# Query block loads moved to the GpSimd queue, and the last sixteen output stores spread over three queues

## The chip, the cores and the metric

The kernel runs on one core of a Trainium2 chip. The metric is the device time of one execution in microseconds (us), and the median of several executions is compared. The engines named below are PE (TensorE; PEld is its weight load), DVE (VectorE), ACT (ScalarE), POOL (GpSimd) and SP (SyncE). SP computes nothing in this kernel: it issues transfers. SPq, ACTq and POOLq are the instruction queues of those engines, on which transfers are issued in program order.

## What is computed

Two blocks in sequence, all in float32. A decayed linear attention over blocks of 64 positions, 4 batches of 8 heads, 768 positions, head dimension 64:

```
intra = einsum('bhic,bhjc->bhij', qb, kb) * Dmask      # Dmask from lam
intra = einsum('bhij,bhjd->bhid', intra, vb)
inter = einsum('bhid,bhde->bhie', qb * lam_pow, kv_state)
out[block] = intra + inter
kv_state = lam_block * kv_state + einsum('bhsd,bhse->bhde', kb * rev_pow, vb)
```

Its output, as 3072 tokens of 512 values, goes through two matrix products with a leaky relu between them:

```
h = x @ w_in                # 512 -> 2048
g = maximum(0.01 * h, h)
y = g @ w_out               # 2048 -> 512
```

The two weights arrive as 64-bit floats and are converted on the chip.

## The kernel before

**Tiling.** The attention is cut in 24 chunks of 128 positions of one batch, 6 chunks to a batch. Four chunks are a group of 512 tokens, so there are six groups. A round (`round_of`, L538) does one chunk: transposes or loads of transposed keys and queries, the scores, the state update, the outputs, and the split of the result in three float32r parts, from which `up` (L697) forms the first product of a group by blocks of 256 columns. Each single float32 product is built of three matmuls on such parts. The results of `up` pass through ACT twice (L727 and L732), are partly combined on DVE (`sums`, L760) and stored to DRAM buffers `g` and `b` (L738, L774) by way of two SBUF buffers `gs`. A buffer `gs` can be written again only when its stores have landed. Later, the second product (L834) reads these DRAM buffers back, and PE runs it from about 310 us to the end.

**Loads of the later chunks.** The first ten chunks (0 to 9) load keys and queries with whole rows (`load_kq`, L339) and transpose them on PE. From chunk `DV` = 10 on, `load_subs` (L371) brings keys and queries of a run of chunks in 32 x 32 blocks, and `turn` (L386) transposes the blocks on DVE (L391). A run is two chunks (10 and 11) or three (12, 15, 18 and 21 onwards), five runs in all. Of each run, keys and queries take 16 transfers each: four indexes `y` of a pair of heads, four quarters `a` of the partitions. One such transfer fills 32 partitions, with pieces of 128 bytes: 48 KB in 384 pieces for a run of three chunks, 32 KB for a run of two. The queries of runs 10, 15, 18 and 21 go to the former query buffer in `att`; those of run 12 to `w32` and `lows`, which other work uses before and after. A run's queries may overwrite the buffer only when `turn` has read the last chunk of the run before. All these loads were issued by SyncE, at L382.

**The order of the work.** The order of each engine's instructions is made by a planner before the program is built (`Plan`, L37). `add` takes an operation with its engine, an assumed duration, keys that it reads and writes, and a rank. `emit` (L83) goes through an assumed time line, always taking the operation that could start first and, among equals, the lowest rank, and issues the instructions in that order. It keeps one assumed clock for each engine, with SP's transfers under the name "DMA". An operation's result counts as available after its duration, a lag for its engine (`LAG`: 3.5 for "DMA", 0.12 for "POOL") and, where `plan.slack` is set, that slack. `move` (L287) adds a transfer to the "DMA" engine with a slack of 1.0 in the earlier part and 4.0 in the steady part (runs 18 and 21 are planned there). In the steady part a block load counts 0.75 (`SUBL`) and before it 0.55. On the chip the instructions of one engine's queue run in this order, and a waiting instruction holds back those behind it.

**The other work of POOL.** In the attention, POOL scales the keys (L427), scales the queries (L431) and decays the state between blocks (L470).

**The output.** `turn_out` (L898) transposes a result bank on DVE (L902) into `otile`, which lies over `gs`, and `store_out` (L905) writes it with four transfers, one for each quarter of the partitions (L910). Before the last bank, these are issued on ACT's queue. At the very end, for the last group, a call is made for banks 2 and 3 (`cs[0]` is 2), both halves `m`, and then, bank 1 being done in two halves, a call for banks 0 and 1 for each half. That is 16 stores of 64 KB, 256 pieces of 256 bytes each. These alternate between SP and ACT.

Of the kernel before, what the change touches and what calls it, by code (L numbers as in the profile page):

```python
# [25 lines left out]
S = 4096.0  # L26
# [5 lines left out]
def _bc(ap, idx, n):  # L32
    a = [list(x) for x in ap.ap]
    return bass.AP(ap.tensor, ap.offset, a[:idx] + [[0, n]] + a[idx:])


class Plan:  # L37
# [23 lines left out]
    def add(self, eng, us, fn, reads=(), writes=(), rank=0.0):  # L61

        n, deps = len(self.ops), set()
        for k in reads:
            w, r = self.last.setdefault(k, [None, []])
            if w is not None:
                deps.add(w)
            r.append(n)
        for k in writes:
            w, r = self.last.setdefault(k, [None, []])  # L70
            if w is not None:
                deps.add(w)
            deps.update(r)
            self.last[k] = [n, []]
        deps.discard(n)
        ways = {eng: us} if isinstance(eng, str) else dict(zip(eng, us))
        if self.slack:
            self.more[n] = self.slack
        if self.chain is not None:
            self.chains[self.chain].append(n)  # L80
        self.ops.append((ways, fn, deps, (self.rank + rank, n), set(writes)))
# [81 lines left out]
def kernel(  # L163
# [10 lines left out]
    nc = tc.nc  # L174
    P = 128
# [18 lines left out]
    SLACK, GSLACK = 4.0, 2.0  # L194
# [5 lines left out]
    LEAD = 8.0  # L200
    WSLACK = 5.0
    DV = 10
    RUNS = {10: (-8.0, 0.8), 12: (4.0, 0.0)}
    C4 = P // 4
    HALF = (slice(0, D), slice(D, 2 * D))
# [72 lines left out]
    plan = Plan()  # L278
    plan.idle, plan.spare, plan.warm = busy, "b10", 1.3 + 0.22 * WARM
    add = plan.add  # L280
    steady = False

    def length(us, issue=0.5):

        return issue if steady else us

    def move(us, fn, reads, writes, issue=0.5, rank=0.0, slack=SLACK):  # L287

        plan.slack = slack if steady else EARLY_SLACK
        if steady and not rank:  # L290
            rank = FIRST
        add("DMA", length(us, issue), fn, reads, writes, rank=rank)
        plan.slack = 0.0


    def factors_k():
        for i in range(2):
            nc.vector.tensor_copy(lam_h[:, i * HP:(i + 1) * HP], lam_b[:, i::2])
        nc.vector.tensor_tensor(eye, ident[:, 0:C2], ident[:, C2:C], op=ALU.add)
        for hi in range(2):  # L300
            for hp in range(HP):
                nc.vector.tensor_tensor_scan(decay[:, hi, hp, :], _bc(lam_h[:, 2 * hp + hi], 1, C2), eye, 0.0,
                                             op0=ALU.mult, op1=ALU.add)
# [9 lines left out]
    lam_c = pow_q[:, :, C2 - 1]  # L313
    plan.rank = -1.0
    add("DVE", 1.95, factors_k, [], ["fk", "sc"])
    add("DVE", 1.25, factors_q, [], ["fq"])
    ENG = {"ACT": nc.scalar, "DVE": nc.vector, "POOL": nc.gpsimd}
# [16 lines left out]
    def of(c):  # L334
        return c // NCB, c % NCB, c % 2
# [3 lines left out]
    def load_kq(c):  # L339
        b, n, i = of(c)  # L340
        for src, x, nm in ((k, 0, "k"), (q, 1, "q")):
            y, dst = src[b, :, n * C:(n + 1) * C, :], kqv[x][i]

            def go(y=y, dst=dst):
                for z in range(2):
                    nc.sync.dma_start(out=dst[:, z * HP:(z + 1) * HP, :], in_=y[z::2].rearrange("h p d -> p h d"))
            if nm == "k" or c < DV:
                move(1.15, go, [], [f"{nm}{i}"], issue=1.0)

    def run(c):  # L350

        lo = max(DV, c - c % TURN)
        return lo, c - c % TURN + TURN - lo

    def subs(first, n):


        n = n * C
        def rows(x, lo, hi):
            return x[:, :(hi - lo) * n].rearrange("p (y t) -> p y t", t=n), lo, hi  # L360
        ks = [(*rows(raw[-2], 0, 2), [f"raw{NRAW - 2}"]), (*rows(raw[-1], 2, 4), [f"raw{NRAW - 1}"])]
        qs = [(*rows(kqv_f[1], 0, HP), ["q0", "q1"])]

        if first == DV:
            ks = [(*rows(raw[0], 0, HP), ["raw0"])]
        elif first < DV + TURN:
            qs = [(*rows(w32f, 0, 2), ["w320", "w321"])] + [
                (*rows(lows[i].bitcast(F32), 2 + i, 3 + i), [f"low{i}"]) for i in range(2)]
        return ks, qs

    def load_subs(c):  # L371
        b, n, i = of(c)
        count = run(c)[1]
        for nm, src, pieces in zip("kq", (k, q), subs(c, count)):
            for sub, lo, hi, keys in pieces:
                add("POOL", 0.0, lambda: None, [], keys, rank=-30.0)
                for y in range(lo, hi):
                    for a in range(4):
                        h = y // 2 + (2 * y + a // 2) % HP * 2
                        z = src[b, h, n * C:(n + count) * C, a % 2 * C4:(a % 2 + 1) * C4]  # L380
                        o = sub[a * C4:(a + 1) * C4, y - lo, :]
                        move(0.55, lambda o=o, z=z: nc.sync.dma_start(  # L382
                                out=o.rearrange("j (m i) -> j m i", i=C4), in_=z.rearrange("(m j) i -> j m i", j=C4)),
                            keys, [f"{nm}s{y}{a}"], issue=SUBL, rank=RUNS.get(c, (4.0, 0.4))[0] + RUNS.get(c, (4.0, 0.4))[1] * (4 * y + a))

# [13 lines left out]
    def transposes(c):  # L399
# [9 lines left out]
        def go(src, at):  # L409
            for y in range(HP):  # L410
                nc.tensor.transpose(out=at[y], in_=src[:, 2 * y:2 * y + 2, :].rearrange("p a d -> p (a d)"), identity=ident)  # L411

        if c < DV:
            add("PE", 0.44, lambda: go(tk, at), [f"k{i}"], [key])
            add("PE", 0.44, lambda: go(tq, [pt[:, y, :] for y in range(HP)]), [f"q{i}"], ["pt"])

        def copies():
            kT = kTs[i]
            into = kT if c < GC else kT.rearrange("p (t a) x -> p t (a x)", t=2)
            src = z if c < GC else z.rearrange("p t a x -> p t (a x)")  # L420
            if c < DV:
                add("ACT", 0.6, lambda: nc.scalar.copy(into, src), [key], [f"kT{i}"])
# [115 lines left out]
    def round_of(c):  # L538

        after = []  # L540
        if c + 2 < NCH:
            load_kq(c + 2)
        plan.begin(c)

        if c < 2 * GC:
            after.append(transposes(c + 2))
        after.insert(0, outputs(c, lambda: after.append(scores(c + 1)) if c + 1 < NCH else None))
        if 2 * GC <= c < NCH - 2:
            after.append(transposes(c + 2))
        plan.end()  # L550
        for x in after:
            x()
        if DV < c + 3 < NCH:
            turn(c + 3)
        if DV + TURN < c + 4 < NCH and (c + 4) % TURN == 0:
            load_subs(c + 4)
        if c + 2 < NCH:
            load_v(c + 2)
# [302 lines left out]
    def plain(pr, p, gi, lead, last=False, banks=None):  # L861
# [20 lines left out]
        for i, c in enumerate(banks):  # L882
            d, b = BANKS[gi][c]
            parts_ = 2 if end and i == 3 else 1
            for half in range(parts_):
                k = ACC[d][b] + (f"half{half}" if parts_ > 1 else "")
                n = T // parts_
                add("PE", 0.227 * 6 * (1.0 if parts_ == 1 else 0.53), lambda c=c, half=half, n=n: go((0, 1), (c,), half * n, n),
                    reads + ([ACC[d][b]] if parts_ > 1 else []), [k])
                turn_out(c, acc[d][b], [ACC[d][b], k], half * n, n)  # L890
                if i == 3 or end and i == 1:
                    cs = sorted(banks[:2] if end and i == 1 else banks[2:] if end else banks)
                    for m in ([half] if parts_ > 1 else range(2)):
                        store_out(pr, gi, m, cs, end)
# [10 lines left out]
    def store_out(pr, gi, m, cs, last):  # L905
        t0, n, w = (2 * pr + m) * T + gi * HT, HT // C4, len(cs) * C4

        def store(a, q):
            c0 = a * P + cs[0] * C4
            q.dma_start(out=out[t0:t0 + HT, c0:c0 + w].rearrange("(b i) j -> i b j", i=C4),  # L910
                        in_=otile[a * C4:(a + 1) * C4, m * n:(m + 1) * n, cs[0]:cs[-1] + 1, :].rearrange("i b c j -> i b (c j)"))

        for a in range(4):
            e = "DMA" if last and (a + m) % 2 else "ACT"
            add(e, 0.5, lambda a=a, e=e: store(a, nc.scalar if e == "ACT" else nc.sync), [f"o{c}{m}" for c in cs], [], rank=-1.5 if last else 6.0)

    def copy_banks(d, s):
        for i in range(2):
# [54 lines left out]
    for n, x in enumerate(seq):  # L973
        plan.rank = float(n)
        steady = begin <= n and x[0] in ("r", "up", "wo")
        if x[0] in "abr":
            {"a": alone, "b": begun, "r": round_of}[x[0]](x[1])
        elif x[0] == "ls":
            load_subs(DV)
            turn(DV)  # L980
        elif x[0] == "lt":
# [59 lines left out]
```

## Time and profile before

| | us |
|---|---|
| median of 3 executions | 606.53 (605.56 to 606.61) |
| the profiled execution, its own time | 606.94 |
| its span, first to last instruction | 605.2 |

All the lines below are of that one profiled execution. Its time is 1.74 us above its span (606.94 - 605.2) and 0.41 us above the median. In the views, a row of the windows gives a stretch of the span, its length, then the busy time of each engine with its count of instructions, the granted TensorE clock (1.00 is full), the mean busy share of the 16 DMA engines and the GB/s moved. A row of the timeline gives the start, the duration, the engine, the line and the operation, with the number of instructions merged, and in brackets how long the engine was idle before it and what ended that. The chain of waits gives start, duration and the work that set the end at that moment.

Of the transfers, `q1` (SP's queue) moved 113.28 MB and `q10` (ACT's) 5.77 MB. No transfer was issued by POOL.

### The profile page before, as it was taken

The page shows a single profiled execution, that of the slowest core. Times are in us where ns is not written, and L with a number is a line of the kernel's source. Part 1 is how long each engine was busy: PE and PEld are TensorE (multiplying, and loading weights), DVE is VectorE, ACT ScalarE, POOL GpSimd, SP SyncE. Part 2 cuts the span into 40 slices and gives each one's busy share as a digit, 9 for nine tenths or more (in the row PEclk, how much of TensorE's full clock was granted, in tenths as well). Part 3 has the DMA queues.
Part 4 walks back from the last instruction along what each step waited for, and adds up shares of the span by engine and source line. Part 5 has one row for each costly group of instructions (what it writes and reads, how often), then busy time and mean ns, then how long its engine had stood idle before and what let it go on. Part 6 is the DMA issues. An engine that isn't in the chain of part 4 may idle for free.

```text
span 605.2 us, 13193 instructions
## 1 busy us (share of the span) xinstructions
PE 589.9 (97%) x5340; PEld 487.4 (81%) x5340; DVE 387.6 (64%) x534; ACT 290.0 (48%) x458; POOL 86.2 (14%) x90
## 2 busy tenths in 40 slices
PE   7899999999999999999999999999999999999996
PEld 6678888888878877887888888888888888888885
DVE  5899765334436327526579858975779595788741
ACT  4678974445555455555577654431344233252300
POOL 1564423104224003202200000000000000000000
PEclk9899999999999999999999999999999999999998
DMA  9999876668899887999879826535467546394533
GB/s 205 226 260 240 254 174 163 158 139 224 207 224 265 216 230 210 216 247 264 266 249 347 260 77 209 167 104 163 148 180 239 176 140 190 121 266 152 174 105 69
DMA packets 190189, 119.89 MB, mean 198 GB/s; under 512 B 128944, under 2 KB 168112, under 8 KB 190128
## 3 DMA queue, kind: packets, MB, share of 16 engines
q1 hardware_dynamic: 176928, 113.28, 66.7%
q10 hardware_dynamic: 13200, 5.77, 3.8%
q8 instruction: 42, 0.69, 0.5%
q14 instruction: 19, 0.16, 0.1%
HBM read 79.17 MB, written 39.85 MB: 197 GB/s over the span
## 4 chain that ended last, share of the span: by engine, by line
PE 89%; DMA 5%; DVE 1%; ACT 1%; SPq 1%; issue 0%; POOL 0%; DVEq 0%; ACTq 0%
PE b L709 38%; PE b L834 13%; PE po L834 13%; PE psc L834 11%; PE pt L834 4%; PE psc L321 4%; PE po L321 4%; DMA b<-gs 2%; DMA raws<-in_moe_w_out_dram 1%; SPq L382 1%; DMA att<-in_v_dram 1%; PE pt L411 1%; DMA att<-in_k_dram 1%; PE po L411 0%; PE b L274 0%
## 5 line engine op out<-in xcount | busy, mean ns | idle before, releaser
L709 PE MATMUL b<-xh,wh 128*128 128x512 f32 (+2 forms) x392 | 103.7, 387 | 2.2 <-ACT gs L732 1.4
L709 PE MATMUL b<-xm,wm 128*128 128x512 f32 (+2 forms) x392 | 104.1, 392 | 1.3 <-ACT b L727 1.3
L709 PE MATMUL b<-xl,wl 128*128 128x512 f32 (+2 forms) x392 | 103.7, 388 | 0.0
L811 ACT ACTIVATE xh<-xm 128x1024 fp32r<-128x1024 f32 x45 | 47.8, 1061 | 91.2 <-DMA xm<-g 39.0
L709 PEld LDWEIGHTS b<-xh,wh 128*128 128x128 f32 x392 | 72.7, 188 | 18.5 <-ACT gs L732 2.7
L709 PEld LDWEIGHTS b<-xm,wm 128*128 128x128 f32 x392 | 71.3, 188 | 17.2 <-ACT b L727 2.5
L709 PEld LDWEIGHTS b<-xl,wl 128*128 128x128 f32 x392 | 72.6, 188 | 14.9 <-DVE wl L614 0.2
L732 ACT ACTIVATE gs<-b 128x512 f32<-128x512 f32 (+2 forms) x97 | 56.9, 590 | 54.3 <-PE b L709 36.5
L727 ACT ACTIVATE b<-b 128x512 f32<-128x512 f32 (+2 forms) x97 | 56.0, 581 | 49.1 <-PE b L709 48.9
L814 DVE SCALAR_TENSOR_TENSOR xl<-xm,xh 128x1024 fp32r<-128x1024 f32 x45 | 54.8, 1218 | 30.8 <-ACT xh L811 26.6
L818 DVE SCALAR_TENSOR_TENSOR xm<-xl,xh 128x1024 fp32r<-128x1024 f32 x48 | 58.7, 1224 | 3.3
L470 POOL TENSOR_TENSOR att<-att 128x256 f32<-128x256 f32 x40 | 34.1, 853 | 54.4 <-DVE att L467 54.4
L602 DVE TENSOR_SCALAR w<-w 128x512 int32<-128x512 int32 x32 | 18.1, 566 | 35.0 <-ACT w L596 34.9
L431 POOL TENSOR_TENSOR att<-att 128x512 f32<-128x512 f32 (+1 forms) x20 | 25.8, 1293 | 95.7 <-DVE att L391 53.5
L460 DVE TENSOR_TENSOR att<-psc,att 128x512 f32<-128x512 f32 x24 | 16.5, 689 | 30.4 <-PE psc L321 30.2
L603 DVE CUSTOM_DVE_ANT_0 w<-w,lows 128x1024 uint16<-128x1024 uint16 x32 | 27.8, 868 | 12.4 <-ACT lows L600 11.2
L321 PEld LDWEIGHTS po<-att 64*64 64x64 f32 x1472 | 27.5, 136 | 8.8 <-issue 5.8
L427 POOL TENSOR_TENSOR att<-att 128x512 f32<-128x512 f32 (+1 forms) x23 | 26.4, 1146 | 57.2 <-DMA att<-in_k_dram 40.2
L321 PE MATMUL po<-att 64*64 64x64 f32 x1472 | 33.2, 224 | 0.6 <-ACT att L499 0.3
L834 PE MATMUL b<-xl,wl 128*128 128x512 f32 (+1 forms) x86 | 33.0, 384 | 0.0
L834 PE MATMUL b<-xm,wm 128*128 128x512 f32 (+1 forms) x86 | 33.0, 384 | 0.0
L834 PE MATMUL b<-xh,wh 128*128 128x512 f32 (+1 forms) x86 | 33.0, 384 | 0.0
(149 smaller groups left out, 1008.2 us busy)
## 6 DMA issues: line engine op xcount, KB each, us to landing
g<-gs SPq DMA_DIRECT2D x31, 512.0 KB, 4.5
xm<-g SPq DMA_DIRECT2D x25, 512.0 KB, 4.5
xm<-b SPq DMA_DIRECT2D x23, 512.0 KB, 3.8
raws<-in_moe_w_in_dram SPq DMA_DIRECT2D x16, 512.0 KB, 5.2
raws<-in_moe_w_out_dram SPq DMA_DIRECT2D x16, 512.0 KB, 5.4
b<-gs SPq DMA_DIRECT2D x16, 512.0 KB, 3.9
att<-in_k_dram SPq DMA_DIRECT2D x48, 128.0 KB, 4.2
att<-in_v_dram SPq DMA_DIRECT2D x24, 256.0 KB, 4.6
```

The lines of the kernel that those rows point to most:

```text
L321: nc.tensor.matmul(dst[HALF[cols]], lhsT=lhsT[HALF[rows]], rhs=rhs[HALF[rows]], start=start, stop=True, skip_group_check=True)
L427: lambda e="POOL": ENG[e].tensor_tensor(kr[nr], kr[nr], _bc(pow_k, 3, D)[nr], op=ALU.mult), ["fk"], [f"k{i}"])
L431: add(eng, us, lambda: e.tensor_tensor(o, x, _bc(pow_q, 2, 2)[:, :, m, :], op=ALU.mult), ["fq", dep], [f"qsT{i}"])
L470: add("POOL", 0.7, lambda new=new, j=j: nc.gpsimd.tensor_tensor(state[(j + 1) % 4], new, _bc(lam_c, 2, D), op=ALU.mult), [f"st{j % 4}", "f ...
L603: add("DVE", 1.0, lambda: nc.vector.tensor_tensor(d, d, low, op=ALU.add), [kl], [key])
L709: nc.tensor.matmul(dst, lhsT=w[z][:, kk * 2 * P + f * P:kk * 2 * P + (f + 1) * P], rhs=x[z][:, kk, toks], start=start and kk == 0, stop=kk ...
L727: add("ACT", ns, lambda b=b: nc.scalar.activation(out=b, in_=b, func=AF.Copy, bias=0.0, scale=S + 1.0), [], [kb], rank=-1.5)
L732: add("ACT", t, lambda o=o, x=s_: nc.scalar.activation(out=o, in_=x, func=AF.Prelu, bias=0.0, scale=(1.0 + 1.0 / S) / (WS * U), alpha=0.01 ...
L811: nc.scalar.activation(out=ring[j][0], in_=g(), func=AF.Copy, bias=0.0, scale=NEAR)
L814: nc.vector.scalar_tensor_tensor(ring[j][1], g(), 1.0, ring[j][0].bitcast(F32), op0=ALU.mult, op1=ALU.subtract)
L818: nc.vector.scalar_tensor_tensor(m, l.bitcast(F32), -S, h.bitcast(F32), op0=ALU.mult, op1=ALU.add)
L834: nc.tensor.matmul(dst, lhsT=lhs(z), rhs=ring[j][z][:, col:col + n], start=first and z == 0, stop=z == 2, skip_group_check=True)
```

## The change

The query part of `load_subs` no longer goes through `move` to SP, but through a new `carry`, which gives it to "POOL" with an assumed duration of 1.0 (`QSL`), a slack of 3.5 - 0.12 + 2.0, and the same rank, keys and addresses. The keys stay on SP. In the last call group of `store_out`, a table says for each quarter `a` which queue issues it: S is SP, A is ACT and P is POOL, with assumed durations 0.5, 0.5 and 0.65.

```diff
+    QSL = 1.0
...
+    def carry(us, fn, reads, writes, issue=0.0, rank=0.0):
+
+        plan.slack = plan.LAG["DMA"] - plan.LAG["POOL"] + GSLACK
+        add("POOL", us, fn, reads, writes, rank=rank)
+        plan.slack = 0.0
...
-                        move(0.55, lambda o=o, z=z: nc.sync.dma_start(
+                        (move if nm == "k" else carry)(0.55 if nm == "k" else QSL, lambda o=o, z=z, e=nc.sync if nm == "k" else nc.gpsimd: e.dma_start(
                                 out=o.rearrange("j (m i) -> j m i", i=C4), in_=z.rearrange("(m j) i -> j m i", j=C4)),
                             keys, [f"{nm}s{y}{a}"], issue=SUBL, rank=RUNS.get(c, (4.0, 0.4))[0] + RUNS.get(c, (4.0, 0.4))[1] * (4 * y + a))
...
+        ENDS = {(8, 0): "PSAP", (8, 1): "PSAP", (4, 0): "SAPP", (4, 1): "SASA"}
+        QUEUES = {"S": ("DMA", 0.5, nc.sync), "A": ("ACT", 0.5, nc.scalar), "P": ("POOL", 0.65, nc.gpsimd)}
...
         for a in range(4):
-            e = "DMA" if last and (a + m) % 2 else "ACT"
-            add(e, 0.5, lambda a=a, e=e: store(a, nc.scalar if e == "ACT" else nc.sync), [f"o{c}{m}" for c in cs], [], rank=-1.5 if last else 6.0)
+            e, us, q = QUEUES[ENDS[8 if cs[0] > 1 else 4, m][a] if last else "A"]
+            add(e, us, lambda a=a, q=q: store(a, q), [f"o{c}{m}" for c in cs], [], rank=-1.5 if last else 6.0)
```

The key (8, m) of the table stands for banks 2 and 3 and (4, m) for banks 0 and 1. So POOL issues four stores of the first eight and two of the last eight, SP and ACT two of the first and three of the last eight each. In all 80 loads (5 runs of 16) and 6 stores go to POOL.

## The prediction
> **What bounds the kernel now.** I read the busy shares first, then the windows, then the places where PE stood idle, and from there the queue of SP.
>
> ```profile
> PE 589.9 (97%) x5340; PEld 487.4 (81%) x5340; DVE 387.6 (64%) x534; ACT 290.0 (48%) x458; POOL 86.2 (14%) x90
> ...
> 60.00:160.00 100.00, 100.00 (x1245) 84.32 (x1244) 50.98 (x87) 58.47 (x103) 27.89 (x28) 1.00 0.76 190
> 160.00:310.00 150.00, 146.98 (x1832) 119.63 (x1832) 72.76 (x139) 81.38 (x147) 30.68 (x33) 1.00 0.87 234
> 172.00:180.00 8.00, 6.97 (x104) 5.34 (x103) 2.48 (x7) 4.91 (x9) 1.17 (x1) 1.00 0.92 251
> 210.00:216.00 6.00, 5.73 (x25) 4.43 (x24) 2.33 (x3) 3.86 (x7) 1.06 (x1) 1.00 0.92 230
> 224.00:232.00 8.00, 6.63 (x147) 4.92 (x146) 4.35 (x10) 4.61 (x9) 0.74 (x1) 1.00 0.69 210
> 310.00:599.30 289.30, 289.30 (x1283) 239.62 (x1281) 214.25 (x226) 109.97 (x138) 0.00 (x0) 1.00 0.57 177
> ```
>
> PE is busy 589.9 of 605.2 us. From 60 to 160 it loses nothing, and from 310 to 599.3, in the second products, nothing either. From 160 to 310, where runs 15, 18 and 21 are loaded, it is busy 146.98 of 150, so 3.02 us are lost. Three windows hold nearly all: 1.03 at 172 to 180, 0.27 at 210 to 216 and 1.37 at 224 to 232, together 2.67; the other 0.35 is scattered. So 3.02 us is the most that the loads can give back. The clock is at 1.00 in all these rows, and nothing is to be had there.
>
> The gaps, and what stands behind them in the chain of waits:
>
> ```profile
> 176.66 1.19 PE L709 MATMUL b<-xm,wm 128*128 128x512 f32 x4 [1.03 <-ACT b L727]
> 214.97 1.20 PE L709 MATMUL b<-xm,wm 128*128 128x512 f32 x4 [0.27 <-ACT b L727]
> 225.53 1.20 PE L709 MATMUL b<-xh,wh 128*128 128x512 f32 x4 [1.20 <-ACT gs L732]
> ...
> 167.55 1.00 SPq L346
> 169.19 5.53 DMA raws<-in_moe_w_out_dram
> 205.50 5.94 DMA b<-gs
> 219.60 5.17 DMA b<-gs
> 224.88 0.04 ACT gs L732
> ...
> b<-gs SPq DMA_DIRECT2D x16, 512.0 KB, 3.9
> ```
>
> At 225.53 PE waits for ACT, ACT for a free `gs`, and that for a store `b<-gs` issued at 219.60, which needs 5.17 us to land. The same at 214.97, with the store of 205.50 that took 5.94. The median of such a store is 3.9, so both were slow as well. The gap at 176.66 is different: ACT waits at the head of its queue for a load of `w_out`, which SP issued at 169.19, behind key loads (L346) that had themselves waited.
>
> Now the queue of SP ahead of the store of 219.60, and when its data were ready:
>
> ```profile
> 216.51 0.47 SPq L382 DMA_DIRECT2D att<-in_q_dram  x1
> 217.03 0.47 SPq L382 DMA_DIRECT2D raws<-in_k_dram  x1
> 217.54 0.47 SPq L382 DMA_DIRECT2D att<-in_q_dram  x1
> ...
> 219.60 0.39 SPq L774 DMA_DIRECT2D b<-gs  x1
> ...
> 216.01 0.43 DVE L766 TENSOR_TENSOR gs<-gs 128x256 f32<-128x256 f32 x1
> ...
> L382 SPq DMA_DIRECT2D att<-in_q_dram x64: 420/469/1813, 72.6 to 272.7; - x64
> ```
>
> DVE had the data at 216.44 (216.01 + 0.43); the store left 3.16 us later. SP was not waiting for anything: it was issuing block loads back to back, one every 0.51 us (217.03 to 217.54), of which two are query loads. That is the bound this change addresses: SP's queue is full here, and urgent stores stand behind loads that have time.
>
> **The change part by part: the loads.** For each run of three chunks 16 issues leave SP, at 0.469 (the median) plus a gap of 0.04 (0.51 - 0.47), so 16 x 0.51 = 8.2 us in the some 40 us that a run lasts. A median is the low side; single ones took up to 1.813. For the store of 219.60 the two query loads between 216.44 and its issue are worth 1.03 us directly; the ones before those had delayed the other loads too, so the bound upwards is the whole 3.16. Even 1.03 leaves only 0.34 of the 1.37 us lost at 224 to 232, and any landing nearer the median (3.9 against 5.17) takes the rest, so I count all 1.37. The store of 205.50 is also behind back-to-back block loads, and 0.27 is less than half of one issue pair: counted in full. The 1.03 at 176.66 I count as staying (0): the load of `w_out` was behind a key load with a wait of its own (1.00 at 167.55), not behind queries. Its ends are 0 and 1.03. The scattered 0.35 also stays. Sum for the loads: -(1.37 + 0.27) = -1.64, with bounds 0 and -3.02.
>
> The planner reckons differently too. In the steady part a query load counted 0.75 + 3.5 + 4.0 = 8.25 until use, and now 1.0 + 0.12 + 5.5 = 6.5 (5.5 rounds 3.5 - 0.12 + 2.0); in the earlier part 0.55 + 3.5 + 1.0 = 5.05 becomes 6.5. So the order on every engine may shift after about 70 us. The trace can't price that; PE's order of matmuls moves little, because it follows ranks, and I count 0.
>
> **What POOL pays.** The trace shows no transfer issued by POOL. The nearest rows are the same transfer on SP below (0.469) and POOL's own instructions above:
>
> ```profile
> L470 POOL TENSOR_TENSOR att<-att x40: 613/626/1607, 11.1 to 293.3; 128x256 f32<-128x256 f32 x40
> L431 POOL TENSOR_TENSOR att<-att x20: 740/1297/2107, 24.4 to 290.5; 128x512 f32<-128x512 f32 x17, 128x256 f32<-128x256 f32 x3
> L427 POOL TENSOR_TENSOR att<-att x23: 1052/1060/1522, 10.1 to 286.8; 128x512 f32<-128x512 f32 x19, 64x512 f32<-64x512 f32 x4
> ...
> 185.13 0.66 DVE L391 STREAM_TRANSPOSE att<-att 128x512 f32<-128x512 f32 x1
> 228.33 0.67 DVE L391 STREAM_TRANSPOSE att<-att 128x512 f32<-128x512 f32 x1
> ...
> 185.80:228.30 42.50, 40.86 (x398) 32.94 (x397) 15.61 (x29) 23.18 (x43) 5.87 (x6) 1.00 0.87 224
> 236.20:276.20 40.00, 40.00 (x399) 32.98 (x397) 16.48 (x33) 22.85 (x41) 6.53 (x8) 1.00 0.93 235
> ```
>
> I bound an issue by 0.47 and 1.30 and take 1.0, nearer to POOL's own medians (0.63, 1.06, 1.30) than to SP's, since it is that engine which will do it. Is there room? Run 18's queries can go once DVE has read the last chunk of run 15 (185.13 + 0.66 = 185.79) and are wanted at 228.33. In these 42.5 us POOL is busy 5.87, so 16 loads may take (42.5 - 5.87) / 16 = 2.3 us each; run 21 has (40.0 - 6.53) / 16 = 2.1. At 1.0 they take 16 of 36.6 us: hidden under POOL's idle time. What stands behind a load on POOL is L427, L431 and the decay L470, which the next round's state products need. One issue delays them by at most 1.0, and the rounds are some 13 us apart (three in the 40 us of a run), so 0 is counted, and 1.0 in the worst placing for each run. Runs 10 and 12 fall in the stretch where PE loses nothing.
>
> A rule speaks against the whole gain. The Trainium skill, page "DMA: Bandwidth & Descriptors", section "Issuing engines are not separate DMA queues", says that transfers of all issuing engines run on the same 16 DMA engines and that another issuer saves only the issue time. By it the long landings (5.17, 5.94) stay, and what is left is the issue time. The row at 185.8 has these engines at 0.87, so the trace agrees in part; that outcome is a rival below.
>
> **The last sixteen stores.**
>
> ```profile
> 598.00:599.00 1.00, 1.00 (x11) 1.00 (x10) 0.66 (x1) 0.00 (x0) 0.00 (x0) 1.00 0.68 137
> 599.00:600.00 1.00, 0.33 (x3) 0.13 (x2) 0.63 (x2) 0.00 (x0) 0.00 (x0) 1.00 1.01 199
> ...
> 602.00:603.00 1.00, 0.00 (x0) 0.00 (x0) 0.00 (x0) 0.00 (x0) 0.00 (x0) 0.50 0.99 195
> 603.00:604.00 1.00, 0.00 (x0) 0.00 (x0) 0.00 (x0) 0.00 (x0) 0.00 (x0) 0.50 0.48 104
> ...
> 597.33 4.60 ACTq L910 DMA_DIRECT2D out_dram<-gs  x8
> 599.37 0.78 DVE L902 STREAM_TRANSPOSE gs<-b 128x256 f32<-128x256 f32 x2 [0.71 <-PE b L834]
> ...
> L910 ACTq DMA_DIRECT2D out_dram<-gs x2: 323/326/330, 601.1 to 601.6; - x2
> DMA to landing us min/median/max: 2.4/2.4/2.5
> ...
> L1036 SPq EVENT_SEMAPHORE  x8: 17/28/155, 603.9 to 605.1; - x8
> ```
>
> The first eight leave from 597.33, the last data are ready at 600.15 (599.37 + 0.78), the last issue starts at 601.6, lands 2.4 later at 604.0, and the closing sequence of SP begins at 603.9. After the change SP and ACT have five each instead of eight, and from 600.15 two each: at 0.47 apiece the last starts by about 600.7 and would land at 603.1, a gain of 0.9. But the DMA engines are full from 599 to 603 (1.01, 0.99), and the bytes stay the same. Only the 0.32 that was idle in 598 to 599 can be filled, so I take -0.3, with 0 and -0.9 as ends. POOL's six must not end later: a store has 256 pieces against a load's 384, so 1.0 x 256 / 384 = 0.67 us; 597.33 + 6 x 0.67 = 601.35, plus 2.4 is 603.75. That just fits. At 0.47 it is never late, at 1.30 it ends at 607.5 and costs 3.6.
>
> A second weighing: that page's section "Latency and other measured facts" puts a transfer's first byte at about 1 us from GpSimd and 0.6 us from the other two. No row of POOL exists; with 0.4 more the six would land at 604.15, and an estimate from this page makes the end 0.25 later than 603.9, and the sum -1.4.
>
> **Sum.** -1.64 - 0.3 = -1.94, about -2.0, on the profiled execution's 606.94: 604.9. The median was 0.41 lower, 606.53, so the prediction for the median is 604.5.
>
> **The rivals.** A measurement of this kernel can tell about 0.2%, 1.2 us, from no change.
>
> *The DMA engines set it, not SP's issuing.* The share is 0.87 from 160 to 310 and up to 0.93 (236 to 276), and SP's issues stretched beyond 0.47 look like pushing against full rings. Then the stores land as late as before. Against it: 3.16 us of delay before the issue is plain queueing. Gain 0 from the loads and 0.3 at the end: 606.2.
>
> *The plan gains more than the relief.* With 80 issues out of SP, the load of `w_out` moves forward too, and all 3.02 us go, with 0.5 at the end: 606.53 - 3.5 = 603.0. For it: SP has no free time at all in these stretches. Against: that load's own wait.
>
> *POOL is too slow for the last stores (the slower side).* Six issues in a row from 597.33 and the landing set the end if one costs over (603.9 + 1.64 - 2.4 - 597.33) / 6 = 0.97 us, from which the gain of the loads is gone. At the upper bound, 1.30, the end is 3.6 later: 606.53 - 1.64 + 3.6 = 608.5. For it: POOL's medians of 1.06 and 1.30. Against: those instructions compute on 65,536 elements, and a store has 256 pieces; by SP's and ACT's 0.33 to 0.47 it would be far off.
>
> *The loads hold up the state decay.* Three runs at 1.0 each, in the worst placing, with the stores' gain: 606.53 + 3.0 - 1.94 = 607.6. Against: the 13 us between rounds.
>
> **How the numbers follow.** Forecast 0.48, full DMA engines 0.15, the larger gain 0.14, slow last stores 0.20, held decay 0.03. The forecast's own range is 603.6 to 605.4; 0.04 of its 0.48 falls above 605.3, within the bound. Faster: 0.44 + 0.14 + 0.02 (of the full engines) = 0.60. Same: 0.04 + 0.13 = 0.17. Slower: 0.20 + 0.03 = 0.23. The range reaches from just under the larger gain, 602.7, to 608.0, into the slow last stores, which leaves out some 0.15 above and 0.04 below.
>
> **What would show it.** Right: SP no longer solid from 186 to 224; the store behind the gap at 225 issued within about 1 us of its data; no PE gap over 0.3 us from 200 to 232; the gap near 176 still there; POOL's busy or issue time up by about 80 us; the DMA share of the last 5 us still near 1. Wrong: stores issued early but landing in 5 to 6 us (full engines); POOL's issues over 1 us, and the closing sequence waiting for one of its stores; new PE gaps ended by POOL's L470 or L427.

## The result, and the profile after

| | us | ratio to before, 95% interval |
|---|---|---|
| before, median | 606.57 | |
| changed, median of 4 (602.58 to 603.61) | 602.80 | 0.9942 [0.9925, 0.9959] |
| changed, measured again beside other runs | 603.43 | 0.9952 [0.9934, 0.9969] |
| the profiled execution of the changed kernel, its own time | 603.61 | |
| its span | 601.8 | |

The change saves 3.8 us against the 2.0 of the forecast. The lines of the kernel are numbered anew: up to the output 7 more than before (L709 is now L716, L382 is L389, L727 and L732 are L734 and L739, L774 is L781), and the output store L910 is L920.

Here are the busy shares, the three queues that transfer, and one row on the first products on PE. That row gives the count, then the shortest, median and longest duration in ns, then the first and the last start in us:

```profile
PE 587.2 (98%) x5340; PEld 486.4 (81%) x5340; DVE 391.1 (65%) x533; ACT 291.7 (48%) x459; POOL 135.6 (23%) x176
...
q1 hardware_dynamic: 146160, 109.40, 62.3%
q10 hardware_dynamic: 12384, 5.58, 3.6%
q0 software_dynamic: 2752, 4.07, 2.7%
...
L716 PE MATMUL b<-xh,wh x392: 220/389/499, 28.7 to 347.4; 128*128 128x512 f32 x188, 128*128 128x384 f32 x4, 128*128 128x128 f32 x4
```

POOL is busy 49.4 us more (135.6 - 86.2): in this view its issues count. The last first product starts at 347.4; in the profile before, the same row reads

```profile
L709 PE MATMUL b<-xh,wh x392: 218/389/500, 30.8 to 351.4; 128*128 128x512 f32 x188, 128*128 128x384 f32 x4, 128*128 128x128 f32 x4
```

So PE is 4.0 us ahead by then and nothing is won or lost afterwards until PE ends. That is at 595.41 (last matmul 595.13 + 0.28) instead of 599.33, 3.92 earlier. From there to the end of the span it takes 6.39 us instead of 5.87: of the 3.92, the last stores give 0.52 back, and 3.4 remain (605.2 - 601.8).

Now the stretch where the three later runs are loaded, in the windows of the changed kernel, and POOL's and SP's timeline there:

```profile
160.00:310.00 150.00, 149.21 (x1848) 123.32 (x1847) 79.67 (x146) 86.11 (x152) 52.02 (x69) 1.00 0.85 239
...
160.00:275.00 115.00, 114.49 (x1536) 94.80 (x1535) 65.65 (x120) 63.81 (x115) 52.02 (x69) 1.00 0.91 249
...
187.34 1.25 POOL L389 DMA_DIRECT2D att<-in_q_dram  x2
190.48 1.30 POOL L438 TENSOR_TENSOR att<-att 128x512 f32<-128x512 f32 x1 [1.89 <-PE po L328]
191.75 0.62 POOL L477 TENSOR_TENSOR att<-att 128x256 f32<-128x256 f32 x1
192.32 1.25 POOL L389 DMA_DIRECT2D att<-in_q_dram  x2
...
L389 POOL DMA_DIRECT2D att<-in_q_dram x64: 584/617/794, 71.7 to 235.1; - x64
```

PE loses 0.79 us of 150 there (3.02 before). A query load costs POOL 0.617 us (the median of the last row), and the loads lie between POOL's own instructions. SP's waits of the whole kernel, after and then before, show that its queue has become looser:

```profile
SPq L745 <- ACT gs L739: 35.2, 17, 4.8
...
SPq L781 <- DVE gs L773: 18.7, 8, 5.6
...
SPq L585 <- ACT lows L607: 16.2, 9, 5.8
```

```profile
SPq L738 <- ACT gs L732: 16.5, 11, 4.8
...
SPq L774 <- DVE gs L766: 8.3, 5, 4.9
...
SPq L578 <- ACT lows L600: 6.4, 5, 2.9
```

The columns are the total us, the times and the longest. In the changed kernel SP stands ready and waits for the data of its stores and for free buffers, some twice as long as before. How long the data waited for SP is in the table behind experiment 6.

### The profile page after: what moved, and what is told of

Its sections match the earlier page's. It is cut to its first block, busy times and chain, and to the rows that moved or that the text cites. A ratio compares the mean times of both kernels' runs of the same rounds, so it can differ in the third digit from the quotient of the medians.

```text
span 601.8 us, 13238 instructions
## 1 busy us (share of the span) xinstructions
PE 587.2 (98%) x5340; PEld 486.4 (81%) x5340; DVE 391.1 (65%) x533; ACT 291.7 (48%) x459; POOL 135.6 (23%) x176
## 3 DMA queue, kind: packets, MB, share of 16 engines
q0 software_dynamic: 2752, 4.07, 2.7%
## 4 chain that ended last, share of the span: by engine, by line
PE 86%; DVE 5%; issue 4%; DMA 2%; SPq 2%; POOL 1%; ACT 1%; POOLq 0%; DVEq 0%; ACTq 0%
PE b L716 40%; PE po L841 12%; PE psc L841 11%; PE b L841 11%; PE pt L841 4%; PE po L328 4%; PE psc L328 3%; SPq L389 1%; DVE w L610 1%; DVE w L609 1%; DMA raws<-in_k_dram 1%; DMA xm<-g 1%; PE pt L418 1%; DMA att<-in_k_dram 1%; DVE att L474 1%
## 5 line engine op out<-in xcount | busy, mean ns | idle before, releaser
L716 PE MATMUL b<-xh,wh 128*128 128x512 f32 (+2 forms) x392 | 103.4, 387 | 1.1 <-ACT xh L522 0.8
L716 PE MATMUL b<-xm,wm 128*128 128x512 f32 (+2 forms) x392 | 104.0, 392 | 0.0
L716 PE MATMUL b<-xl,wl 128*128 128x512 f32 (+2 forms) x392 | 103.2, 387 | 0.6 <-DVE wl L621 0.6
L716 PEld LDWEIGHTS b<-xh,wh 128*128 128x128 f32 x392 | 72.9, 188 | 16.3 <-ACT xh L522 0.9
L716 PEld LDWEIGHTS b<-xl,wl 128*128 128x128 f32 x392 | 72.8, 188 | 15.7 <-DVE wl L621 1.0
L716 PEld LDWEIGHTS b<-xm,wm 128*128 128x128 f32 x392 | 71.5, 188 | 14.9
L734 ACT ACTIVATE b<-b 128x512 f32<-128x512 f32 (+2 forms) x97 | 56.2, 581 | 55.6 <-PE b L716 55.5
L739 ACT ACTIVATE gs<-b 128x512 f32<-128x512 f32 (+2 forms) x97 | 57.2, 592 | 48.7 <-PE b L716 40.1
L920 POOL DMA_DIRECT2D out_dram<-gs x6 | 3.5, 588 | 319.3 <-issue 319.3
L477 POOL TENSOR_TENSOR att<-att 128x256 f32<-128x256 f32 x40 | 33.7, 841 | 38.0 <-DVE att L474 37.9
L438 POOL TENSOR_TENSOR att<-att 128x512 f32<-128x512 f32 (+1 forms) x20 | 24.5, 1223 | 71.4 <-PE po L328 50.0
L389 POOL DMA_DIRECT2D att<-in_q_dram x64 | 39.7, 625 | 3.0 <-DVE att L398 1.7
L610 DVE CUSTOM_DVE_ANT_0 w<-w,lows 128x1024 uint16<-128x1024 uint16 x32 | 29.8, 930 | 7.5 <-ACT lows L607 6.1
```

The costliest lines, as they stand in the source:

```text
L389: (move if nm == "k" else carry)(0.55 if nm == "k" else QSL, lambda o=o, z=z, e=nc.sync if nm == "k" else nc.gpsimd: e.dma_start(out=o.rea ...
L477: add("POOL", 0.7, lambda new=new, j=j: nc.gpsimd.tensor_tensor(state[(j + 1) % 4], new, _bc(lam_c, 2, D), op=ALU.mult), [f"st{j % 4}", "f ...
L610: add("DVE", 1.0, lambda: nc.vector.tensor_tensor(d, d, low, op=ALU.add), [kl], [key])
L716: nc.tensor.matmul(dst, lhsT=w[z][:, kk * 2 * P + f * P:kk * 2 * P + (f + 1) * P], rhs=x[z][:, kk, toks], start=start and kk == 0, stop=kk ...
L734: add("ACT", ns, lambda b=b: nc.scalar.activation(out=b, in_=b, func=AF.Copy, bias=0.0, scale=S + 1.0), [], [kb], rank=-1.5)
L739: add("ACT", t, lambda o=o, x=s_: nc.scalar.activation(out=o, in_=x, func=AF.Prelu, bias=0.0, scale=(1.0 + 1.0 / S) / (WS * U), alpha=0.01 ...
```

## The experiments

Three theories were put against each other. *Queue*: SP's issue time held back the urgent stores and loads. *Order*: the planner, having 80 issues less for SP, makes a better order. *Engines*: POOL's transfers come in fewer packets and free the DMA engines. A change of `load_subs` is shown against the changed kernel. "Stores as before" means this line:

```diff
-            e, us, q = QUEUES[ENDS[8 if cs[0] > 1 else 4, m][a] if last else "A"]
+            e, us, q = QUEUES["S" if last and (a + m) % 2 else "A"]
```

The kernel before was measured again beside each group of runs: its median was 607.81 beside runs 1 to 4, 606.47 beside runs 5 to 7 and 607.14 beside runs 8 to 10. So kernels are compared within a group, or by their ratio to the kernel before, given with its 95% interval. Beside runs 1 to 4 the kernel before spread from 606.57 to 611.39 us; the ratios of these four lie up to 0.002 below the quotients of the medians, and are best compared with each other.

**1. The loads alone** (stores as before).

> The changed kernel with the last sixteen stores issued by SP and ACT as before; only the query loads are on POOL. Before 606.6, changed 602.8. The changed kernel's profile has PE ending 3.9 us earlier, but 6.39 us from there to the end instead of 5.87. If the spread stores cost that 0.5 us, this run is at 602.3. If they gain the 0.3 us of the prediction, it is at 603.1. If the loads bring no more than the 1.64 us of the prediction's sum, it is at 605.0.

603.11 us, 0.9905 [0.9878, 0.9931]. PE, DVE and ACT do the sequence of the changed kernel, and the whole gain is there: it comes from the loads. In the profile of this run PE ends at 595.07 and the span is 601.0: 5.93 from there to the end, as before.

**2. The stores alone** (all block loads on SP as before).

```diff
-                        (move if nm == "k" else carry)(0.55 if nm == "k" else QSL, lambda o=o, z=z, e=nc.sync if nm == "k" else nc.gpsimd: e.dma_start(
+                        move(0.55, lambda o=o, z=z, e=nc.sync: e.dma_start(
```

> The kernel before with only the last sixteen stores spread over SP, ACT and POOL. Stores cost 0.5 us: 607.1. The prediction's 0.3 us gain, DMA engines full from the first store on: 606.3. Issue time alone sets the end: 605.7.

609.04 us, 1.0013 [0.9994, 1.0031]: no gain, and by the interval not surely a loss. The profile has 6.84 us from PE's end (600.66) to the end of the span (607.5), 0.97 more than before.

**3. The order of before, POOL issuing** (stores as before).

```diff
-                        (move if nm == "k" else carry)(0.55 if nm == "k" else QSL, lambda o=o, z=z, e=nc.sync if nm == "k" else nc.gpsimd: e.dma_start(
+                        move(0.55, lambda o=o, z=z, e=nc.sync if nm == "k" else nc.gpsimd: e.dma_start(
```

> The query loads planned as before, as transfers of SP, so that the order of the work on every engine is that of the kernel before, but issued by POOL; stores as before. Queue theory (SP's issue time held back the urgent stores): most of the gain is here, 603 to 604.5, with the gap of 1.03 us at 176 still there and those at 215 and 225 gone. Order theory (the planner's new order is what gains): 606.0 to 606.6. Engine theory (POOL's transfers come in fewer, larger packets and free the DMA engines): also 603 to 604.5, but then with landings of the stores to b nearer 3 us than before's 3.9 median.

602.18 us, 0.9888 [0.9859, 0.9917]. The order theory falls: PE, DVE, ACT and POOL's own work follow exactly the sequence of before, and the gain is all there. One half of the expectation was wrong as well: the gap of 1.03 at 176 is gone. The timeline of SP here, and of ACT and PE behind it:

```profile
163.94 2.29 SPq L353 DMA_DIRECT2D att<-in_k_dram  x2
166.32 0.58 SPq L585 DMA_DIRECT2D raws<-in_moe_w_out_dram  x1
...
172.30 0.58 ACT L734 ACTIVATE b<-b 128x512 f32<-128x512 f32 x1 [0.25 <-PE b L716]
172.79 0.65 ACT L603 ACTIVATE w<-raws 128x512 f32<-128x512 f32 x1
...
175.73 1.07 PE L716 MATMUL b<-xm,wm 128*128 128x512 f32 x4
176.63 1.07 PE L716 MATMUL b<-xl,wl 128*128 128x512 f32 x4
```

The key loads leave at 163.94 instead of 167.41, the load of `w_out` at 166.32 instead of 169.19, and ACT no longer stands idle for it. The landing of the stores to `b` stayed at a median of 3.9 us, which speaks against the engine theory. (That of the stores to `g`, over the whole kernel, went from 4.5 to 4.1; in the stretch that matters it did not, see the table behind experiment 6.)

**4. The order of the changed kernel, SP issuing** (stores as before).

```diff
-                        (move if nm == "k" else carry)(0.55 if nm == "k" else QSL, lambda o=o, z=z, e=nc.sync if nm == "k" else nc.gpsimd: e.dma_start(
+                        (move if nm == "k" else carry)(0.55 if nm == "k" else QSL, lambda o=o, z=z, e=nc.sync: e.dma_start(
```

> The query loads planned as in the changed kernel, as POOL's work, so that the order of PE, DVE and ACT is that of the changed kernel, but issued by SP at the places the plan gives; stores as before. Queue theory: SP is as full as before, 605.5 to 608. Order theory: 602.5 to 603.5. Engine theory: 605.5 to 608 as the queue theory, since the packets are small again; this run tells order from the other two.

615.85 us, 1.0111 [1.0081, 1.0141], slower than any theory had it, and the order theory's 602.5 to 603.5 is ruled out again. The order that the planner makes for an SP without the queries makes the kernel about 8 us longer (615.85 against 607.81) if SP has to issue them after all. Its windows have

```profile
160.00:275.00 115.00, 106.03 (x1361) 86.75 (x1360) 57.90 (x109) 57.02 (x104) 26.93 (x30) 0.96 0.86 221
```

PE loses 9 of 115 us there. The granted clock in this row is 0.96, where every other kernel has 1.00 in this window, so a part of the 8 us is slower matmuls; how much wasn't separated. Runs 1, 3 and 4 and the kernel before make a table of two orders and two queues: with POOL issuing both orders are good (0.9905, 0.9888), and with SP issuing the one of before is better (1 against 1.0111).

**5. ACT issuing, order of before** (stores as before). This tells queue from engines: ACT's queue is of SP's kind, `hardware_dynamic` in the rows below, with the small packets.

```diff
-                        (move if nm == "k" else carry)(0.55 if nm == "k" else QSL, lambda o=o, z=z, e=nc.sync if nm == "k" else nc.gpsimd: e.dma_start(
+                        move(0.55, lambda o=o, z=z, e=nc.sync if nm == "k" else nc.scalar: e.dma_start(
```

> Order of the kernel before, query loads issued by ACT at the places where SP had them, stores as before. ACT issues by the same kind of queue as SP, so the packets stay small. Queue theory: SP is as free as with POOL, and the time is 602 to 604.5 plus what 80 issues of 0.47 us and their waits cost on ACT's own queue (48% busy); anything below 606 supports it. Engine theory (large packets of POOL's transfers free the DMA engines): no gain, 606 to 612.

601.99 us, 0.9926 [0.9907, 0.9946]. The windows and the queues of this kernel:

```profile
160.00:275.00 115.00, 115.00 (x1369) 95.10 (x1372) 54.88 (x108) 65.24 (x116) 23.94 (x26) 1.00 0.91 240
...
q1 hardware_dynamic: 146976, 109.60, 62.2%
q10 hardware_dynamic: 43152, 9.45, 7.7%
```

PE is busy in all 115 us, while the DMA engines are at 0.91, against 0.89 before in the same window: fuller, and the gain is whole. The large packets of POOL are not needed.

**6. The engines relieved, SP's queue kept** (order and queue of before, stores as before). Of the 384 pieces of a query load (256 in the run of two chunks) 32 are fetched. The kernel leaves the rest of the queries out, and clears the part of the buffer that no load fills once at the start.

```diff
-                        (move if nm == "k" else carry)(0.55 if nm == "k" else QSL, lambda o=o, z=z, e=nc.sync if nm == "k" else nc.gpsimd: e.dma_start(
-                                out=o.rearrange("j (m i) -> j m i", i=C4), in_=z.rearrange("(m j) i -> j m i", j=C4)),
+                        move(0.55, lambda o=o, z=z, e=nc.sync, s=slice(None) if nm == "k" else slice(0, 1): e.dma_start(
+                                out=o.rearrange("j (m i) -> j m i", i=C4)[:, s], in_=z.rearrange("(m j) i -> j m i", j=C4)[:, s]),
```

> Order and queue of the kernel before, but each query block load fetches 32 of its 384 pieces (one of three runs' columns of 32 positions); the other eleven twelfths of the block are left out, and the part of the buffer that no load fills is cleared once at the start. The DMA engines lose nearly all the work of the query loads, SP keeps its 80 issues. Engine theory: 602 to 603.5. Queue theory: 604.5 to 606.5, since SP still issues as many, each perhaps shorter than 0.47 us; if the issues shrink to 0.35 us a part of the gain comes by that way, and the profile shows it.

603.06 us, 0.9943 [0.9926, 0.996]: a good part of the gain, more than the queue theory allowed, and inside what the engine theory said.

```profile
160.00:275.00 115.00, 114.43 (x1301) 93.82 (x1301) 54.34 (x107) 63.55 (x113) 24.55 (x26) 1.00 0.80 224
...
L390 SPq DMA_DIRECT2D att<-in_q_dram x64: 310/469/1859, 72.1 to 267.0; - x64
```

The median issue is unchanged at 0.469, though a load has a twelfth of its pieces. But all of SP's issues that start between 160 and 275, added up from the trace, take 88.9 us here, against 97.0 before and 70.0 in the changed kernel. The query loads have no part in that (25.0 us for 40 of them, 23.5 for 41 before): the other issues take 63.9 instead of 73.6, and only 16 of all last over 1 us, instead of 24. So with emptier engines (0.80 for 0.89) the long issues get fewer, and 8 us off SP's 97 go with most of the gain.

Did the stores leave sooner, or land sooner? The traces tell. For the 11 stores `b<-gs` that start between 160 and 300 us (10 in run 4), the table has the mean time from the end of the DVE instruction that made the data to the start of the store's issue, and from there to the landing; then the landing of the stores `g<-gs` of the same stretch; then what PE lost from 160 to 305 us (the count by starts, explained in the next section; in run 4 with the lower clock). All are us, added up from the traces.

| | before | changed | run 3 | run 4 | run 5 | run 6 |
|---|---|---|---|---|---|---|
| `b<-gs`: data ready to issue | 3.38 | 1.05 | 1.29 | 3.64 | 1.80 | 2.50 |
| `b<-gs`: issue to landing | 4.05 | 4.46 | 4.22 | 3.79 | 3.94 | 3.83 |
| `g<-gs`: issue to landing | 4.80 | 5.07 | 4.83 | 4.97 | 4.73 | 4.68 |
| lost by PE | 6.6 | 2.4 | 2.4 | 9.6 | 2.6 | 3.6 |

Wherever time was gained the wait in front of SP's issue fell; the landing moved by some 0.4 us at most, up as often as down. In run 4, the slow one, the wait stayed, though these stores landed soonest. In run 6 too the wait fell by 0.88 us and the landing by 0.22: for these stores, relieving the engines worked mainly by way of SP's queue. Full engines are one cause of a full queue, then, and nothing here shows them as a bound of their own in this stretch.

**7. Each query load in two halves on POOL** (order of before, stores as before), 160 issues.

```diff
-                        (move if nm == "k" else carry)(0.55 if nm == "k" else QSL, lambda o=o, z=z, e=nc.sync if nm == "k" else nc.gpsimd: e.dma_start(
-                                out=o.rearrange("j (m i) -> j m i", i=C4), in_=z.rearrange("(m j) i -> j m i", j=C4)),
+                        move(0.55, lambda o=o, z=z, e=nc.sync if nm == "k" else nc.gpsimd, w=count * 4: [e.dma_start(
+                                out=o.rearrange("j (m i) -> j m i", i=C4)[:, s], in_=z.rearrange("(m j) i -> j m i", j=C4)[:, s])
+                                for s in ([slice(0, w)] if e is nc.sync else [slice(0, w // 2), slice(w // 2, w)])],
```

> Order of the kernel before, query loads issued by POOL, each split in two of half the columns: 160 issues instead of 80. POOL's share is hidden under its idle time: about the time of the old order with 80 issues on POOL (0.9888 of before, 602.2), within 0.7 us. If POOL's issuing or its order of work were close to the bound, each run's 16 further issues of about 0.6 us (10 us in 40) would show as new gaps on PE ended by POOL, 604 and more.

602.37 us, 0.9934 [0.9909, 0.9958], with no new gap on PE. An issue of half the size took 0.567 us (median of 128), so POOL spent nearly twice the time, and it cost nothing.

**8. The order of before on POOL again.**

> Order of the kernel before, query loads issued by POOL, stores as before, once more beside the two runs below. 0.9888 of before in its first call, where before was spread widely; with 80 issues by ACT 0.9926, split in 160 by POOL 0.9934. Expected here 0.990 to 0.9935, about 602.3, and so 0.5 to 1 us below the changed kernel.

602.48 us, 0.9923 [0.9905, 0.994]. This ratio is the better one for this kernel: the 0.9888 of run 3 stood beside the widely spread runs of before.

**9. The keys on POOL too** (order of before, stores as before).

```diff
-                        (move if nm == "k" else carry)(0.55 if nm == "k" else QSL, lambda o=o, z=z, e=nc.sync if nm == "k" else nc.gpsimd: e.dma_start(
+                        move(0.55, lambda o=o, z=z, e=nc.gpsimd: e.dma_start(
```

> As above, with the key block loads on POOL as well: 160 issues of 0.62 us. If SP's queue is no longer a bound once the queries are gone, nothing more is to be had: within 0.6 us of the old order with queries on POOL. If SP is still a bound, 0.5 to 1.5 us less. If POOL's queue is now the full one (each run 32 issues, 20 us of 40, beside 6 us of its own work), new gaps ended by POOL and some us more.

603.91 us, 0.995 [0.9932, 0.9967], some 1.4 us above run 8 (603.91 - 602.48). One wait of PE between 60 and 310 us is not there in run 3. Its total, the chain of waits that leads to it, and the window around it:

```profile
PE po L328 <- DVE att L506: 1.3, 1, 1.3
...
158.98 4.17 DMA raws<-in_k_dram
163.27 0.45 DVE att L398
163.72 0.06 DVE att L506
163.82 0.46 PE po L328 x16
...
160.00:165.00 5.00, 3.72 (x135) 3.00 (x134) 1.73 (x6) 2.86 (x5) 4.98 (x9) 1.00 1.01 264
```

PE waits for a small copy on DVE (L506), which stands behind the transpose of a block of keys (L398), and that waits for a key load which POOL issued at 158.98 and which landed 4.17 us later. POOL is busy 4.98 of the 5 us from 160 on, issuing key and query loads in turn. So now POOL's queue is the full one, and a key load that is wanted soon stands among query loads that have time. That is the third case of the expectation, in a small way.

**10. POOL issuing two of the last sixteen stores** (order of before, query loads on POOL). Both are of the first eight.

```diff
-        ENDS = {(8, 0): "PSAP", (8, 1): "PSAP", (4, 0): "SAPP", (4, 1): "SASA"}
+        ENDS = {(8, 0): "PSAS", (8, 1): "PASA", (4, 0): "SASA", (4, 1): "SASA"}
```

> Order of the kernel before, query loads issued by POOL, and of the last sixteen stores POOL issues two, both of the first eight; SP and ACT issue seven each. In the changed kernel POOL's six stores reach the DMA engines 1.5 us after their issue and the time from the end of PE to the end is 6.39 us, against 5.85 without POOL. If POOL's late start is what costs, two early stores are harmless and save two issues: 5.4 to 5.9 us after the end of PE. If any store by POOL costs (large packets in the way of the others), 6.1 to 6.4.

602.63 us, 0.9928 [0.991, 0.9947]. From PE's end (594.87) to the end of the span (600.7) 5.83 us: two early stores on POOL cost nothing and gain nothing, where six cost 0.5 to 1 in the profiles of the changed kernel and of run 2.

The changed kernel was measured again beside runs 5 to 7:

> The changed kernel once more, beside the runs of this call. Ratio to before 0.9942 in its first measurement. The loads alone were 0.9905 and the old order with POOL issuing 0.9888 in another call; if the spread stores really cost the 0.5 us that the profiles show, it lies 0.5 us above the loads alone; if the two calls differ by the chip alone, its ratio is about 0.991 here.

603.43 us (603.16 to 604.16). ACT issuing (601.72 to 602.41) and the halves on POOL (601.55 to 603.08), both with the stores as before, lie wholly below it. The best version found keeps the order and the stores of before and lets ACT or POOL issue the query loads: 602.0 to 602.5, about 1 us below the changed kernel. Run 1 against run 3 points at the order (603.11 and 602.18, new and old order with the same stores), the ends of the profiles at the stores; their shares weren't separated.

## Why the prediction was right, and where its sizes were off

**The time.** The measured 602.80 lies below the forecast's own range, 603.6 to 605.4, and nearest to the rival of the larger gain, 603.0. That rival fits partly by luck. It had the load of `w_out` moving forward, which came true. But it had 3.02 us from the loads and 0.5 gained at the end, where the profiles have 3.92 gained and 0.5 lost.

**The bound: right.** SP's queue held back stores whose data were ready. Runs 3 and 5 show it with the order of the work unchanged, by two other queues, and run 4 from the other side. In the table behind experiment 6 the stores' wait in front of SP's issue falls from 3.38 us to 1.05, and their landing doesn't get shorter.

**The signs.** Of the six that were to show the forecast right, two came: SP was less solid from 186 to 224 (30.6 us of issues, 34.2 before), and no gap of PE from 200 to 232 was over 0.3 us (one of 0.37 in this kernel's second profile). The gap near 176 did not stay, POOL's time rose by 49 us and not 80, and the DMA share at the end fell to 0.55 in one window. And the store behind the gap at 225, the fifth of the table's 11, still left 3.63 us after its data in the changed kernel, now at 216.97. There it is the stores up to 186 us and from 238 to 278 that left at once, and in the planner's new order PE did not stop for the fifth. In run 3, with the order of before, it left 0.19 us after its data.

**"So 3.02 us is the most that the loads can give back": wrong.** PE was 3.92 us earlier at its end. The bound was read from PE's idle time, and a busy matmul row hides part of a pause. The rows of before:

```profile
212.73 1.07 PE L709 MATMUL b<-xh,wh 128*128 128x512 f32 x4
213.64 1.07 PE L709 MATMUL b<-xl,wl 128*128 128x512 f32 x4
214.97 1.20 PE L709 MATMUL b<-xm,wm 128*128 128x512 f32 x4 [0.27 <-ACT b L727]
```

Four matmuls start every 0.91 us (213.64 - 212.73), 0.227 each, though one row lasts 0.39. The next was due at 214.55 and started at 214.97: 0.42 late, of which 0.27 is shown as idle. Every pause hides up to 0.16 in this way (0.39 - 0.227), and shorter ones don't show at all. And the matmul after it is followed 0.34 us later, not 0.227 (its row of four lasts 1.20 and not 1.07). So a pause here costs some 0.27 more than its shown idle time. Counted by starts, that is the time from one 512-column matmul to the next start beyond 0.227, summed over 160 to 305 us, PE lost 6.6 us before, 2.4 in the changed kernel and 2.4 in run 3.

**The sum of the loads, -1.64: the term that was mis-sized.** Run 3 has PE's sequence of before, so every matmul can be set beside itself. From 160 to 310 us PE gains 4.4 us there: 1.30 at the gap of 176.66, which was counted 0; 0.54 at 214.97, counted 0.27; 1.47 at 225.53 and 0.44 at 227.82, together counted 1.37; 0.35 at 276.63, where the row shows only 0.07 idle; the rest is scattered. Two things were wrong. The gaps were counted by their shown idle time, as above. And "The 1.03 at 176.66 I count as staying (0)" was wrong: the load of `w_out` stood behind key loads with a wait of their own, but those stood in the same full queue. With the queries gone and the order unchanged it left 2.9 us earlier (169.19 to 166.32, run 3), and the gap went.

**The planner's new order, counted 0: right, as far as it goes.** With POOL issuing, the order of before is as good or better (runs 1 and 3). The reason given, that PE's order moves little, was not so good: some 650 of PE's 5340 instructions stand elsewhere in the order.

**POOL's price: taken as 1.0, measured 0.617; and its cover held.** The bounds 0.47 and 1.30 held too. The count of room, up to 2.1 us a load, was not contradicted by the query loads: twice the issues cost nothing (run 7). But room in the sum says nothing of one load's place in the queue, as run 9 shows. What stands behind a load on POOL, L434, L438 and L477, made no new gap in the profile of run 3 or 7.

**The last stores, -0.3: wrong in sign.** An issue cost POOL 0.584 us (0.67 was taken), and its sixth was issued when SP's and ACT's last were. Not counted was the start. In the trace of the changed kernel POOL's first store begins 0.60 us after SP's first, and its first packet follows 1.56 us after the issue began, where SP's first packet follows after 0.85. So the DMA engines have less to do in the middle and are late at the end. POOL's stores are not the last to land, as the forecast had it: its sixth landed at 600.06. But the last of SP and of ACT landed at 600.51 and 600.68, 3.7 and 3.8 us after their issues began, where the forecast took 2.4. The windows from PE's end on, the changed kernel first, then run 1 with the stores as before:

```profile
595.00:596.00 1.00, 0.41 (x4) 0.21 (x2) 0.55 (x2) 0.00 (x0) 1.00 (x3) 1.00 0.99 203
596.00:597.00 1.00, 0.00 (x0) 0.00 (x0) 0.23 (x1) 0.00 (x0) 1.00 (x3) 1.00 0.55 136
597.00:598.00 1.00, 0.00 (x0) 0.00 (x0) 0.00 (x0) 0.00 (x0) 0.49 (x1) 0.78 0.89 189
```

```profile
595.00:596.00 1.00, 0.07 (x1) 0.00 (x0) 0.78 (x2) 0.00 (x0) 0.00 (x0) 1.00 0.94 178
596.00:597.00 1.00, 0.00 (x0) 0.00 (x0) 0.00 (x0) 0.00 (x0) 0.00 (x0) 1.00 1.07 229
597.00:598.00 1.00, 0.00 (x0) 0.00 (x0) 0.00 (x0) 0.00 (x0) 0.00 (x0) 0.78 0.94 183
```

The DMA share drops to 0.55 in the second window of the changed kernel and stays near 1 without POOL's stores. The prediction had the engines as the bound of this end, rightly, and then let POOL's stores join them without delay. Run 10 fits: two stores, early, are harmless. That the late start and not the kind of packet costs is argued from these windows and run 10; the two weren't separated. In medians the 0.5 us can't be told from no change (run 2, 0.9994 to 1.0031). In the profiles it can: from PE's end to the end of the span the three with six stores on POOL take 6.2 to 6.8 us, the ten others 5.6 to 6.0.

**The rival of full DMA engines** was half right. The Trainium skill's rule ("DMA: Bandwidth & Descriptors", section "Issuing engines are not separate DMA queues"), that another issuer saves only issue time, agrees with the trace: in the table the stores to `b` and `g` land no sooner in the changed kernel (4.46 and 5.07 us, 4.05 and 4.80 before). But issue time was what was short. And relieving the engines alone also helped (run 6), mainly by way of that issue time. The same page of the Trainium skill, section "Latency and other measured facts", has the first byte about 0.4 us later from GpSimd (about 1 us, against 0.6). The packets above show 0.7 (1.56 - 0.85), in the same sense, with the DMA engines already at work on the stores of SP and ACT.

## What to carry to other kernels

A queue that issues without a pause delays what is urgent by its backlog. Here 8% less issue time in the stretch went with most of the gain (run 6). Move the transfers that have time to a queue with idle time, and only those: with the keys as well, the other queue was the full one (run 9). A new order of the work was not needed for the gain. Count PE's losses by the starts of its matmuls, not by idle time. At the very end, put the stores on the queues whose packets start soonest; that rests on the profiles of this case alone.

## What was not expected of the hardware

POOL's transfers are cut in other packets: 86 of them made 2752 packets, 32 each, for 4.07 MB, while ACT's 80 loads in run 5 added some 30,000 (43152 - 13200). An issue on POOL depended little on its pieces: a median of 0.567 us for 192 of 128 bytes (run 7), 0.617 for 384. SP's issue of a twelfth of the pieces took as long, 0.469, as that of all (run 6), while ACT issued the full loads in 0.318 (median of 64, run 5).
